# Moving block 0's query bound, the dense blocks' first transposes and the last block's start in a one-core transformer block

## The chip, the core and the metric

One core of a Trainium2 chip runs the kernel. Its engines have their own instruction streams, each executed in order, and wait for each other by semaphores: PE (TensorE, matrix products, with PEld as its weight loads), ACT (ScalarE), DVE (VectorE), POOL (GpSimd) and SP, which here issues most transfers. SBUF holds 128 partitions of data, and PSUM, in banks of 512 float32 per partition, takes what PE computes. The metric is the time of one execution on the device, in microseconds (us); the median of the runs is compared.

## What is computed

A transformer block on one sequence of 2048 tokens and 512 features, in float32: normalization, attention with 32 heads of 16 features that share one key and one value head, a residual, a second normalization and a gated feed-forward part (1792 inner features) with another residual.

```python
B, S, D, H, F = 1, 2048, 512, 32, 1792
q = (x @ wq).reshape(B, S, H, Dh).transpose(0, 2, 1, 3); k = x @ wk; v = x @ wv
p = softmax(einsum("bhqd,bkd->bhqk", q, k) * Dh ** -0.5)
o = einsum("bhqk,bkd->bhqd", p, v)          # heads side by side, then @ wo
h  = x + A(layernorm(x))                    # A: the lines above
h2 = h + (gelu(ln(h) @ w_gate) * (ln(h) @ w_up)) @ w_down
```

## The kernel before

**Precision.** Float32 operands are split into a rounded part and a rest (`split`, L106: the rounded copy, tile `...hi` or `...h`, then by a DVE subtraction the rest, `...lo` or `...l`), and a product is a sum of three PE products: high by high, high by low, low by high.

**Attention** runs over 4 blocks of 512 queries (b). In each, 8 groups (g) of 4 heads; in each group 16 chunks of 128 keys. For each key chunk there are two *scores*, numbered n in the program's order over everything (256 a block): a score is two PE matmuls into one of two PSUM tiles `s` (L329) and one exponential of 128x1024 on ACT, `p<-s` (L333). Two scores fill one tile p, which is numbered i = n // 2. `weigh` (L335) multiplies p with the values into the accumulator `acc` (eight PE instructions in the trace for each p), of which there is one: at the end of a group DVE copies it to `oT` (L350), and the next group's first `acc` waits for that copy. `oT` goes to DRAM, comes back transposed as `oc`, and is divided on DVE. Instead of a maximum, the softmax takes a bound: a row of the query operand holds m, computed from the norms of the queries and keys.

**Block 0** also computes the queries of all blocks (`project_q`, L170, a generator). Its loop (L800) goes over n; in every *cycle* of four scores it asks the generator for one step: `yield 3` is three products `pq`, and after a block's twelve such groups and their copies on DVE (`qh`, `ql`, `qs`) there is a sum of squares `pqn` (L218). Then DVE copies `qn` and takes its maximum `q2` (L223), in a later step POOL makes two factors `mm` (L227), and in another DVE makes the bound `m` and SP stores it (L245). These products share a single PSUM bank. While `work` is there (`given`, L809), the products of p with the values follow two at a time at the end of a cycle; without it, one by one (`finish(1)` at n % 4 == 2: the *plain* rhythm). The bound of the first heads of block 0 is made in the prologue (`urgent`). POOL meanwhile splits the dense weights and stores them to DRAM (`part_weights`).

**The dense part** of block b runs during the attention of block b + 1, as a generator too (`dense`, L517). The loop over chunks of 5 or 6 scores (L846) takes its steps by the table `kinds`: four "long" chunks for the output projection, one "gap", then the long ones of the feed-forward part. `start` (L570) makes the output projection `pp` for rows 0 and 1, then for rows 2 and 3 (a row is 128 tokens), with the transposes of row 0 in between. `residual` (L551) adds x to form `h`, takes the statistics (`st`, `mv`), POOL makes 1/sqrt (`rstd`, L120-121) and DVE the normalized `xn`; `x_transpose` (L562) transposes on PE into a bank `pxt`, from which `split` makes `x2h` and `x2l`. The first products of the feed-forward part, `pg` and `pu`, read all four rows of `x2h`. `duo` (L480) computes two products at once, each on half of the array's rows. Here three PSUM banks serve the products.

**The last block** has no attention to run beside: `start_tail` (L594) uses five further PSUM banks (`tail_bank`, L504) and full products (`solo`, L507). It interleaves its start with the last down products of block 2 (L899-909); the normalization takes a `shift` from POOL and runs on ACT (`on_act` in `layer_norm`, L113-131).

ACT, PE and POOL (L135) and, in the loops, SP and DVE keep the order in which the program writes their instructions.

Of the kernel before, what the change touches and what calls it, by code (L numbers as in the profile page):

```python
# [14 lines left out]
ALU = mybir.AluOpType  # L15
# [27 lines left out]
def kernel(  # L43
# [69 lines left out]
    def layer_norm(sb, xn, src, key, on_act=False):  # L113

        st = sb.tile([P, 6], F32, tag="st", bufs=4, name=f"st_{key}")
        mv = sb.tile([P, 2], F32, tag="mv", bufs=4, name=f"mv_{key}")
        nc.vector.bn_stats(st, src)
        nc.vector.bn_aggr(mv, st)  # L118
        rstd = sb.tile([P, 1], F32, tag="rstd", bufs=4, name=f"rstd_{key}")
        nc.gpsimd.tensor_scalar(rstd, mv[:, 1:2], EPS, None, op0=ALU.add)  # L120
        nc.gpsimd.tensor_tensor(rstd, rstd, power[:, 0:1], op=ALU.pow)
# [6 lines left out]
        nc.gpsimd.tensor_scalar(  # L128
            shift, mv[:, 0:1], rstd, -1.0, op0=ALU.mult, op1=ALU.mult
        )  # L130
        return partial(nc.scalar.activation, xn, src, AF.Identity, bias=shift, scale=rstd)
# [9 lines left out]
    def run(outer, first):  # L141
# [28 lines left out]
        def project_q(b, cs, eng, col):  # L170
# [46 lines left out]
            for i, c in enumerate(cs):  # L217
# [6 lines left out]
            yield 2  # L224

            mm = eb.tile([H, 3], F32, tag="mm", bufs=2, name=f"mm_{b}_{cs[0]}")
            nc.gpsimd.tensor_scalar(  # L227
                mm[:, 0:1], q2[:, col : col + 1], k2m, 1e-30, op0=ALU.mult, op1=ALU.add
            )
            nc.gpsimd.tensor_tensor(mm[:, 1:2], mm[:, 0:1], power[:H, 0:1], op=ALU.pow)  # L230
            nc.gpsimd.tensor_scalar(
                mm[:, 2:3], mm[:, 0:1], mm[:, 1:2], 0.5, op0=ALU.mult, op1=ALU.mult
            )
            nc.gpsimd.tensor_scalar(
                mm[:, 1:2], mm[:, 1:2], k2m, 0.5, op0=ALU.mult, op1=ALU.mult
            )
# [8 lines left out]
            nc.vector.tensor_scalar(m, qn, mm[:, 1:2], mm[:, 2:3], op0=ALU.mult, op1=ALU.add)  # L245
            hs = slice(cs[0] * HC, (cs[-1] + 1) * HC)
            nc.sync.dma_start(q_d[hs, 3 * DH, tsl].bitcast(F32), m[hs].bitcast(F32))
            yield 2

        ms = {}  # L250
# [3 lines left out]
        def later_q():  # L254
            second = project_q(1, range(DC), nc.vector, 1)
# [10 lines left out]
            check_bound(eb, k2m)  # L266
# [250 lines left out]
        def dense(b, tail=False):  # L517

            o_hi, o_lo = o_blk[b]
            eng = nc.scalar if tail else nc.vector  # L520
# [30 lines left out]
            def residual(t0):  # L551
# [7 lines left out]
                for scale in scaled:  # L559
                    scale()  # L560

            def x_transpose(t):  # L562
                bank = tail_bank if tail else psum1
                pt = bank(f"pxt_{b}_{t}").rearrange("p (c q) -> p c q", c=DC)
                for c in range(DC):
                    nc.tensor.transpose(pt[:, c, :], xns[t][:, c * P : (c + 1) * P], ident)  # L566
                sl = slice(t * P, (t + 1) * P)
                split(eng, xT_hi[:, :, sl], xT_lo[:, :, sl], pt)

            def start():  # L570
                yield from project(0)
                residual(0)
# [3 lines left out]
                second, turned = project(2), 0  # L576
                while True:
                    n = next(second, None)
                    if n is None:
                        break  # L580
                    if n == CUT:
                        yield EDGE
                        x_transpose(0)
                        turned = 1
                    yield n
                for t in range(turned, 2):
                    x_transpose(t)
                residual(2)
                yield GAP
                x_transpose(2)  # L590
                x_transpose(3)
                yield CUT

            def start_tail():  # L594
# [39 lines left out]
                for t in range(1, TB):  # L634
                    norm(t)
                for t in range(TB - 1):
                    scaled[t]()
                yield HOLD
                x_transpose(0)
                scaled[TB - 1]()  # L640
                x_transpose(1)
                yield 3
                x_transpose(2)
                x_transpose(3)
# [104 lines left out]
        gates = []  # L749
# [43 lines left out]
        with tc.manual_schedule(engines={mybir.EngineType.SP, mybir.EngineType.DVE}):  # L793
            parts = None
# [5 lines left out]
            while n < lead:  # L800
# [45 lines left out]
        for c in range(LEAD[0], (NB - 1) * NG * len(SIZES)):  # L846
# [18 lines left out]
            for j, share in enumerate(shares):  # L865
# [23 lines left out]
            finish(sum(e[5] < n - 1 for e in pend) if cg < len(SIZES) - 1 else len(pend))  # L889
            if outs:  # L890
# [337 lines left out]
```

## Time and profile before

| what | value |
|---|---|
| median of 3 runs | 1466.33 us (1466.04 to 1467.09) |
| profiled execution, its own time | 1464.85 us |
| its span, first to last instruction | 1462.9 us |
| DVE busy | 538.5 us (37%) |
| POOL busy | 222.2 us (15%) |
| PE in the chain that ended last | 76% of the span |
| ACT in that chain | 16% |

The profile is of one execution. A busy time is the time in which an engine had an instruction under way. A row of a timeline has start, duration, engine, line of the kernel, operation, tiles out<-in without their numbers, shape, count, and in brackets how long the engine had been idle and which instruction of which engine ended that. A window's row has its borders and length, then busy time and count for PE, PEld, DVE, ACT and POOL, and last the granted share of PE's clock, the share of the DMA engines in use and their GB/s. Where only some instructions are asked for, the engines without any are left out. The chain that ended last is followed back from the last instruction, at each step to what released it.

### The profile page before, as it was taken

To read this page: it belongs to the slowest core of one execution; us is meant where nothing else is said; L and a number is where in the kernel's file an instruction comes from. 1 tells how busy PE (TensorE), PEld (TensorE's weight loads), DVE (VectorE), ACT (ScalarE), POOL (GpSimd) and SP (SyncE) were. 2 spreads that over 40 slices of the span, in tenths; PEclk is the share of its full clock that TensorE was granted. 3 is DMA by queue.
4 is the path that set the end of the run, shared out by engine and by line. 5 is a ranking of instruction groups with operands and counts; after the bars stand their busy time and mean duration, and the time that the engine had idled before them with its cause. 6 is when DMAs were issued, how large, how long until landed. Compare 5 with 4: busy or idle time off the path is not lost.

```text
span 1462.9 us, 24764 instructions
## 1 busy us (share of the span) xinstructions
PE 1413.6 (97%) x10420; PEld 748.4 (51%) x10420; DVE 538.5 (37%) x925; ACT 1040.0 (71%) x1147; POOL 222.2 (15%) x305
## 2 busy tenths in 40 slices
PE   6999999999999999999999999999899999999998
PEld 5533333334555555554555555554455555556886
DVE  7412231313251424333251423423242332426665
ACT  6699999996777777776777777777677777772000
POOL 5477677611000000000000000000000000001000
PEclk9999999999999999999999999999999999999999
DMA  4465766641323332212332332203333232333552
GB/s 153 150 202 192 223 219 221 213 151 60 116 92 105 113 112 84 85 56 98 129 108 88 113 112 84 84 30 113 112 113 112 84 112 75 126 120 112 199 183 81
DMA packets 58863, 180.54 MB, mean 123 GB/s; under 512 B 8540, under 2 KB 8540, under 8 KB 51544
## 3 DMA queue, kind: packets, MB, share of 16 engines
q1 hardware_dynamic: 48912, 144.79, 29.1%
q0 software_dynamic: 9760, 34.08, 7.0%
q8 instruction: 84, 1.38, 0.4%
q14 instruction: 35, 0.29, 0.1%
q10 hardware_dynamic: 72, 0.00, 0.0%
HBM read 131.13 MB, written 47.71 MB: 122 GB/s over the span
## 4 chain that ended last, share of the span: by engine, by line
PE 76%; ACT 16%; DVE 3%; issue 3%; POOL 1%; DMA 0%; SPq 0%; ACTq 0%; POOLq 0%; DVEq 0%
PE acc L337 32%; PE s L329 17%; ACT p L333 16%; PE pd L490 5%; PE pu L490 5%; PE pg L490 4%; PE pq L180 3%; PE pg L512 3%; PE pd L512 3%; PE pu L512 3%; PE pp L490 1%; PE pxt L566 0%; PE pk L1015 0%; DVE x2h L110 0%; DVE x2l L111 0%
## 5 line engine op out<-in xcount | busy, mean ns | idle before, releaser
L333 ACT ACTIVATE p<-s 128x1024 f32<-128x1024 f32 x1024 | 969.2, 1042 | 274.4 <-PE s L329 273.9
L337 PE MATMUL acc<-p,v_sb 128*32 128x512 f32 x4096 | 492.8, 599 | 4.4 <-DVE oT L350 4.4
L329 PE MATMUL s<-qg,kaug 50*128 50x512 f32 x1984 | 394.9, 437 | 18.6 <-ACT p L333 15.1
L329 PEld LDWEIGHTS s<-qg,kaug 50*128 50x128 f32 x1984 | 170.9, 184 | 307.7 <-ACT p L333 192.0
L337 PEld LDWEIGHTS acc<-p,v_sb 128*32 128x32 f32 x4096 | 111.0, 109 | 247.1 <-issue 232.8
L490 PE MATMUL pg<-x2h,w 64*128 64x512 f32 x672 | 231.7, 391 | 3.0 <-DVE x2h L110 3.0
L490 PE MATMUL pu<-x2h,w 64*128 64x512 f32 x672 | 231.8, 391 | 0.0
L120 POOL TENSOR_SCALAR rstd<-mv 128x1 f32<-128x1 f32 x16 | 3.5, 218 | 1018.4 <-DVE mv L118 1018.2
L490 PEld LDWEIGHTS pg<-x2h,w 64*128 64x128 f32 x672 | 124.7, 186 | 15.2 <-DVE x2h L110 4.2
L490 PE MATMUL pg<-x2l,w 64*128 64x512 f32 x336 | 131.5, 391 | 0.7 <-DVE x2l L111 0.7
L490 PE MATMUL pu<-x2l,w 64*128 64x512 f32 x336 | 131.5, 391 | 0.0
L490 PEld LDWEIGHTS pu<-x2h,w 64*128 64x128 f32 x672 | 124.7, 186 | 11.1
L490 PE MATMUL pd<-w,gh 64*128 64x512 f32 x672 | 105.4, 391 | 0.0
L679 ACT ACTIVATE ga<-ga 128x512 f32<-128x512 f32 x56 | 36.2, 647 | 87.9 <-DVE ga L674 87.9
L671 DVE COPY g<-pg 128x512 f32<-128x512 f32 x56 | 38.5, 688 | 126.7 <-PE pg L490 121.1
L490 PEld LDWEIGHTS pd<-w,gh 64*128 64x128 f32 x672 | 63.3, 185 | 14.7 <-issue 0.7
L680 DVE SCALAR_TENSOR_TENSOR ga<-ga,g 128x512 f32<-128x512 f32 x56 | 38.8, 692 | 79.8 <-ACT ga L679 79.8
L490 PEld LDWEIGHTS pg<-x2l,w 64*128 64x128 f32 x336 | 62.3, 186 | 9.1 <-DVE x2l L111 1.6
L490 PE MATMUL pd<-w,gl 64*128 64x512 f32 x336 | 66.5, 392 | 0.0
L490 PEld LDWEIGHTS pu<-x2l,w 64*128 64x128 f32 x336 | 62.3, 186 | 7.3
L498 DVE COPY mark_pu<-pu 128x1 f32<-128x1 f32 x42 | 6.6, 158 | 159.3 <-PE pu L490 159.3
L707 DVE TENSOR_TENSOR h<-h,pd 128x512 f32<-128x512 f32 x48 | 30.8, 684 | 90.2 <-PE pd L490 90.2
(226 smaller groups left out, 1307.3 us busy)
## 6 DMA issues: line engine op xcount, KB each, us to landing
w<-w_d SPq DMA_DIRECT2D x84, 1024.0 KB
qg<-q_d SPq DMA_DIRECT2D x62, 200.0 KB
q_d<-qh SPq DMA_DIRECT2D x32, 256.0 KB
acc_d<-oT SPq DMA_DIRECT2D x32, 256.0 KB
oc<-acc_d SPq DMA_DIRECT2D x128, 64.0 KB
w_d<-w_0b POOLq DMA_DIRECT2D x14, 512.0 KB, 5.9
w_d<-w_1b POOLq DMA_DIRECT2D x14, 512.0 KB, 3.5
x<-in_A_x_dram SPq DMA_DIRECT2D x16, 256.0 KB
```

The lines of the kernel that those rows point to most:

```text
L120: nc.gpsimd.tensor_scalar(rstd, mv[:, 1:2], EPS, None, op0=ALU.add)
L180: nc.tensor.matmul(pq, wt[:, d, c * P : (c + 1) * P], xt[:, d, :], start=(n == 0), stop=(n == 3 * DC - 1),)
L329: nc.tensor.matmul(s[:, a, :], kaug[rows, kc * P : (kc + 1) * P], qg[rows, u, :], start=True, stop=True,)
L333: nc.scalar.activation(p[:, 2 * u : 2 * u + 2, :], s, AF.Exp, scale=SCALE)
L337: nc.tensor.matmul(acc[32 * j : 32 * j + 32, :], v_sb[:, kc, :], p[:, j, :], start=(kc == 0), stop=(kc == KC - 1), skip_group_check=True,)
L490: nc.tensor.matmul(banks[k], lhsT[rows], rhs[rows], start=(turn == 0 and i == 0), stop=(turn == 1 and i == n - 1), skip_group_check=True,)
L498: nc.vector.tensor_copy(mark, banks[1][:, :1])
L512: nc.tensor.matmul(bank, lhsT, rhs, start=(i == 0), stop=(i == len(ts) - 1))
L671: nc.vector.tensor_copy(g, pg)
L679: nc.scalar.activation(a, a, AF.Tanh, scale=GELU_A * GELU_C)
L680: nc.vector.scalar_tensor_tensor(a, a, 1.0, g, op0=ALU.add, op1=ALU.mult)
L707: nc.vector.tensor_tensor(hs[t], hs[t], pd, op=ALU.add)
```

## The change

Three things are moved; all products and exponentials stay.

- **Block 0.** `project_q` hands the factors and the bound of a later block to a list `after`, with the number of steps after which each is due (2 and 4, counted from the step of the sum of squares, which counts as the first), and goes on with the next products at once. `later_q` works the list off behind the products. `given` falls when the products have ended, not when the bound has.
- **Start of the dense part, blocks 0 to 2.** DVE's work on rows 2 and 3 (`residual(2)`) comes before the split of row 1, and the scaling to `xn` and that split wait in a list `behind` until the chunk's last weighing has been written (and with it, at a group's end, the copy to `oT`). The transposes of rows 2 and 3 stand behind the second score of the gap chunk instead of its end, and DVE makes both `x2h` before both `x2l`.
- **Start of the last block.** `shift` is a DVE instruction ahead of the scaling; row 2's transpose takes a bank of the other pool; `x2h` of rows 0 and 1 goes from ACT to DVE; the copies of `pp` into `h` come earlier on ACT, two of them between the scalings.

```diff
@@ layer_norm
-        nc.gpsimd.tensor_scalar(
-            shift, mv[:, 0:1], rstd, -1.0, op0=ALU.mult, op1=ALU.mult
-        )
-        return partial(nc.scalar.activation, xn, src, AF.Identity, bias=shift, scale=rstd)
+        def scale():
+            nc.vector.scalar_tensor_tensor(
+                shift, mv[:, 0:1], -1.0, rstd, op0=ALU.mult, op1=ALU.mult
+            )
+            nc.scalar.activation(xn, src, AF.Identity, bias=shift, scale=rstd)
+        return scale
@@ project_q
             nc.vector.tensor_reduce(q2[:, col : col + 1], qn, axis=AX.X, op=ALU.max)
-            yield 2
...
             if urgent:
+                yield 2
+                factors()
...
-            yield 0
-            nc.vector.tensor_scalar(m, qn, mm[:, 1:2], mm[:, 2:3], op0=ALU.mult, op1=ALU.add)
...
+            after.extend([[2, factors], [4, bound]])
             yield 2
@@ later_q
+            for said in later_products():
+                for entry in after:
+                    entry[0] -= 1
+                while after and after[0][0] <= 0:
+                    after.pop(0)[1]()
+                yield said
+            while after:
+                yield 0
+                after.pop(0)[1]()
+                yield 0
+            check_bound(eb, k2m)
@@ dense: residual, x_transpose
-                for scale in scaled:
-                    scale()
+                return scaled
...
-            def x_transpose(t):
-                bank = tail_bank if tail else psum1
+            def x_turn(t):
+                bank = tail_bank if tail and t != 2 else psum1
...
-                split(eng, xT_hi[:, :, sl], xT_lo[:, :, sl], pt)
+                if tail and t >= 2:
+                    first_part = partial(nc.scalar.activation, hi, pt, AF.Copy)
+                else:
+                    first_part = partial(nc.vector.tensor_copy, hi, pt)
+                return first_part, partial(
+                    nc.vector.tensor_tensor, lo, pt, hi.bitcast(F32), op=ALU.subtract
+                )
@@ dense: start
-                for t in range(turned, 2):
-                    x_transpose(t)
-                residual(2)
+                parts = x_turn(1)
+                behind.extend([*residual(2), *parts])
                 yield GAP
-                x_transpose(2)
-                x_transpose(3)
+                two = [x_turn(t) for t in (2, 3)]
+                for i in range(2):
+                    for parts in two:
+                        parts[i]()
                 yield CUT
@@ dense: start_tail
-                for t in range(1, TB):
-                    norm(t)
-                for t in range(TB - 1):
-                    scaled[t]()
+                scaled[0]()
+                out(0)
+                norm(1)
+                norm(2)
+                scaled[1]()
+                out(1)
+                norm(3)
+                scaled[2]()
                 yield HOLD
-                x_transpose(0)
-                scaled[TB - 1]()
-                x_transpose(1)
+                parts = x_turn(0)
+                parts[0]()
+                scaled[3]()
+                parts[1]()
+                for part in x_turn(1):
+                    part()
                 yield 3
...
-                for t in range(TB):
-                    nc.scalar.activation(hs[t], pps[t], AF.Copy)
+                out(2)
+                out(3)
@@ the loops
-                    given = work is not None
-                for _ in range(RAMP.get(n, n > 7 and n % 4 == 3) if given else 0):
-                    if next(work, None) is None:
-                        work = None
+                    given = work is not None and said > 0
+                for _ in range(RAMP.get(n, n > 7 and n % 4 == 3) if work is not None else 0):
+                    said = next(work, 0)
+                    if said == 0 and not after:
+                        drain()
...
+                if kind == "gap" and j == 1:
+                    said = next(work)
...
             finish(sum(e[5] < n - 1 for e in pend) if cg < len(SIZES) - 1 else len(pend))
+            while behind:
+                behind.pop(0)()
```

More of the change, by code (lines that the diff above doesn't have):

```diff
@@ L575, in start @@
                 yield CUT
[L576 to L580, printed above, removed]
+                second = project(2)
+                for n in second:
                     if n == CUT:
                         yield EDGE
-                        x_transpose(0)
-                        turned = 1
+                        for part in x_turn(0):
+                            part()
                     yield n
-                for t in range(turned, 2):
-                    x_transpose(t)
-                residual(2)
+                parts = x_turn(1)
+                behind.extend([*residual(2), *parts])
                 yield GAP
-                x_transpose(2)
-                x_transpose(3)
+                two = [x_turn(t) for t in (2, 3)]
+                for i in range(2):
+                    for parts in two:
+                        parts[i]()
                 yield CUT
@@ L747, in finish @@
                     evacuate(pb, pg, pacc)
-        gates = []
+        gates, behind = [], []
         def open_gates():
@@ L793, in run @@
         with tc.manual_schedule(engines={mybir.EngineType.SP, mybir.EngineType.DVE}):
-            parts = None
+            parts, said = None, 3
             if first:
```

48 lines of the change are left out of this document (30 added, 18 removed).

## The prediction

> **What bounds the kernel now.** I read the page first: its busy shares, then its costliest group.
>
> ```profile
> PE 1413.6 (97%) x10420; PEld 748.4 (51%) x10420; DVE 538.5 (37%) x925; ACT 1040.0 (71%) x1147; POOL 222.2 (15%) x305
> L333 ACT ACTIVATE p<-s 128x1024 f32<-128x1024 f32 x1024 | 969.2, 1042 | 274.4 <-PE s L329 273.9
> ```
>
> Through three quarters of the chain of waits PE is the last to finish. The exponentials (ACT) wait 273.9 us for scores, and one takes 1.04 us. The change adds no PE work and removes none, so only time in which PE waits, or runs at less than its rate, can be won. It lies in three places.
>
> First block 0, by the busy times of three windows: a stretch of loop cycles with a product, one without products in the rhythm that goes with them, one after the products.
>
> ```profile
> 205.96:271.11 65.15, 65.15 (x434) 24.98 (x433) 14.66 (x19) 60.35 (x65) 49.43 (x57) 1.00 0.67 220
> 275.27:287.17 11.90, 9.54 (x74) 3.10 (x74) 5.12 (x9) 11.31 (x13) 7.42 (x11) 1.00 0.52 183
> 291.47:320.38 28.91, 28.91 (x196) 8.45 (x192) 0.69 (x1) 28.91 (x33) 7.88 (x10) 1.00 0.33 111
> ```
>
> The windows run from the start of one exponential to the start of another, so the ACT counts hold one too many: 64, 12 and 32 exponentials. Four of them (one cycle) take 65.15/16 = 4.07 us with a product and PE busy throughout, 11.90/3 = 3.97 us in the empty cycles, where PE is busy 9.54 of 11.90 us, and 28.91/8 = 3.61 us in the plain rhythm, where ACT is always busy.
>
> Second, the first dense block's start in blocks 1 to 3. PE in block 2, in order of time (start, duration, idle before):
>
> ```profile
> 683.02 0.39 PE L490 MATMUL pp<-wo_hi,o_lo 64*128 64x512 f32 x2
> 683.34 0.65 PE L566 MATMUL pxt<-ident,xn 128*128 128x128 f32 x4
> 683.92 2.78 PE L337 MATMUL acc<-p,v_sb 128*32 128x512 f32 x24
> 686.63 0.73 PE L329 MATMUL s<-qg,kaug 50*128 50x512 f32 x4
> 690.65 1.41 PE L337 MATMUL acc<-p,v_sb 128*32 128x512 f32 x8 [1.82 <-DVE oT L350]
> 693.14 2.17 PE L337 MATMUL acc<-p,v_sb 128*32 128x512 f32 x8
> 695.67 1.09 PE L566 MATMUL pxt<-ident,xn 128*128 128x128 f32 x8
> 698.43 0.49 PE L490 MATMUL pg<-x2h,w 64*128 64x512 f32 x1 [1.00 <-DVE x2h L110]
> 699.50 0.39 PE L490 MATMUL pg<-x2h,w 64*128 64x512 f32 x1
> ```
>
> DVE beside it:
>
> ```profile
> 684.03 0.69 DVE L110 CAST x2h<-pxt 128x512 fp32r<-128x512 f32 x1 [6.47 <-PE pxt L566]
> 685.36 1.28 DVE L554 TENSOR_TENSOR h<-pp,xb 128x512 f32<-128x512 f32 x2
> 688.45 0.55 DVE L560 TENSOR_SCALAR xn<-h,mv,rstd 128x512 f32<-128x512 f32 x1 [0.20 <-POOL rstd L121]
> 689.45 0.55 DVE L560 TENSOR_SCALAR xn<-h,mv,rstd 128x512 f32<-128x512 f32 x1 [0.46 <-POOL rstd L121]
> 689.91 0.68 DVE L350 COPY oT<-acc 128x512 f32<-128x512 f32 x1
> ```
>
> PE waits three times: for the copy oT that stands last on DVE, then for the split of the late transposes (x2h), and in between it runs slowly, 2.17 us for the eight matmuls of acc.
>
> Third, the last block's start, where the third and fourth transposes wait for x2l (rows below).
>
> **Block 0.** The bound of the queries leaves the cycle of the products. Counted in the order of instructions, before has nine cycles without a product: two behind each of four sums of squares, and one more at the end, which all keep the rhythm of the products. After moves every later product up into these; one empty cycle is left, and the last eight, after the products, get the plain rhythm. The products themselves cost 4.07 us wherever they stand. So the gain is 9 x 3.97 - (3.97 + 8 x 3.61) = 2.9 us; the transition costs the same, wherever it comes: I take 2.8. Bounds: 3.2 (nine plain cycles), 2.0 (a third of it lost to a changed DVE order).
>
> What moves with it: on SP, each load of qg now follows one group of three stores of qh more or less than before. It is wanted seven cycles (7 x 4.07 = 28 us) after it is issued, so this is covered. On POOL the four instructions of the bound stand two to five weight parts earlier; they may hold the parts up, but POOL's 7.88 us in the third window above are the last of them, and their reader, the dense products, comes later. On DVE the bound itself now stands ahead of product copies, which is the slow rival below.
>
> **The start of the dense block.** Block 2 in the new order. DVE adds h first, when the products end (683.02 + 0.39 = 683.41): 683.45 in place of 685.36, 1.91 earlier. By the old distances (3.09 and 4.09 us from h to the two xn, POOL's part included) the xn could start at 686.54 and 687.54. But oT is now ahead of them and waits for acc, which ends at 683.92 + 2.78 = 686.70: oT 686.74 to 687.43, xn to 687.98 and 688.50. The transposes of both, which before followed five scores later, now stand in PE's order behind the second score, which ends at 686.63 + 0.73 = 687.36. So PE waits 0.7 us, works on them until 689.15 (0.65 us after the second xn), and the scores behind them are 0.8 us later than before. But now oT is done, and so are x2h and x2l: six DVE operations of 0.69 us from 688.5, by 692.7. Five more scores follow, at the pace of the exponentials, which I take as 1.06 us each with small waits (0.91 is the plain rhythm): 689.1 + 5.3 = 694.4 for the first gate product pg. Before, the third pair of products starts at 699.50; without the waits of the first two pairs, and 0.23 us for each pair, that is a start of 699.04. The gain is 4.6 us. Bounds: 5.4 at 0.91 us for a score, 2.9 at 1.4, the pace with a wait for acc at each score.
>
> Block 3 is the same stretch: from the scores to the third pair 12.91 us against block 2's 12.87, so 4.6 again.
>
> ```profile
> 1024.06 0.73 PE L329 MATMUL s<-qg,kaug 50*128 50x512 f32 x4
> 1036.97 0.39 PE L490 MATMUL pg<-x2h,w 64*128 64x512 f32 x1
> ```
>
> In block 1 the gap falls inside a group of heads, with no oT in it:
>
> ```profile
> 354.10 0.40 PE L490 MATMUL pp<-wo_hi,o_lo 64*128 64x512 f32 x2
> 358.93 0.75 PE L329 MATMUL s<-qg,kaug 50*128 50x512 f32 x4
> 367.96 0.39 PE L490 MATMUL pg<-x2h,w 64*128 64x512 f32 x1
> ...
> 357.09 1.28 DVE L554 TENSOR_TENSOR h<-pp,xb 128x512 f32<-128x512 f32 x2
> 361.18 0.55 DVE L560 TENSOR_SCALAR xn<-h,mv,rstd 128x512 f32<-128x512 f32 x1 [0.45 <-POOL rstd L121]
> ```
>
> h moves from 357.09 to 354.55, the second xn from 361.18 to 358.64, before the score at 358.93 is done (0.5 us): the transposes run from 359.45 to 360.5 (1.09), four scores follow, pg starts at 360.5 + 4 x 1.06 = 364.7 in place of 367.96 - 0.46 = 367.5. Gain 2.8; bounds 3.4 (0.91) and 1.4 (1.4).
>
> **The clock in the gap.** Windows of 3.41 us, a pair of each block; the third number from the end of a row is the granted clock:
>
> ```profile
> 687.84:691.25 3.41, 1.09 (x10) 0.34 (x10) 2.07 (x5) 2.28 (x3) 1.49 (x3) 1.00 0.00 0
> 691.25:694.67 3.42, 3.42 (x18) 0.87 (x12) 0.00 (x0) 1.85 (x2) 0.00 (x0) 0.50 0.34 119
> 1025.76:1029.17 3.41, 1.59 (x12) 0.44 (x12) 1.69 (x3) 1.79 (x2) 1.00 (x3) 1.00 0.08 32
> 1029.17:1032.58 3.41, 3.41 (x12) 0.72 (x12) 0.00 (x0) 1.94 (x2) 0.00 (x0) 0.50 0.31 107
> 363.57:366.98 3.41, 2.40 (x18) 1.24 (x14) 2.08 (x4) 1.73 (x3) 0.00 (x0) 1.00 0.00 0
> 366.98:370.39 3.41, 3.19 (x26) 2.47 (x28) 0.59 (x1) 1.75 (x3) 0.00 (x0) 1.00 0.02 5
> ...
> 363.57:366.98 3.41, 1.09 (x8) 0.85 (x8) 1.00 0.00 0
> ```
>
> After a window with PE busy 32% (block 2) or 47% (block 3) the clock is halved for the next one. In block 1, busy 70% (the last row counts its transposes alone, 1.09 us), it stays whole. My new gap holds idle PE of 0.7, 0.45 and 0.55 us in 7 us, over 65% busy in any 3.41 us, so I count it at the full clock.
>
> The Trainium skill speaks against that: "TensorE: Matmul & The Clock Gate", Part 4, says that a transpose does not count as PE work for the clock in the way other matmuls do; Part 1, that an idle window of about 3.4 us halves the clock. Block 1's row disagrees on the first: without transposes it is (2.40 - 1.09)/3.41 = 38% busy, less than block 3's 47%, and kept the clock. By that rule the new gap would be near 50% and might be halved again, and the sum 3.4 us less.
>
> **The last block's start.** PE, then ACT and DVE:
>
> ```profile
> 1335.85 1.46 PE L566 MATMUL pxt<-ident,xnp 128*128 128x128 f32 x8
> 1339.18 0.66 PE L566 MATMUL pxt<-ident,xnp 128*128 128x128 f32 x4 [0.98 <-DVE x2l L111]
> 1341.96 0.50 PE L512 MATMUL pg<-x2h,w 128*128 128x512 f32 x1
> ...
> 1337.13 0.78 ACT L637 ACTIVATE xnp<-pp,shift,rstd 128x512 f32<-128x512 f32 x1 [0.54 <-POOL shift L128]
> 1333.35 0.29 DVE L111 TENSOR_TENSOR o_lo<-oc,o_hi 128x128 fp32r<-128x128 f32 x1
> ```
>
> The third transpose waits for a bank that x2l frees; after gives it a bank of another pool, and it starts behind its xn (337.13 + 0.78, some 0.2 later by the shift on DVE: 1338.1) and the down products, at 1338.35. The fourth waits for its xn, whose shift now stands behind a DVE copy of x2h: xn 1338.25 to 1339.03, transpose to 1339.7, x2h on ACT to 1340.35, pg at 1340.5. The gain is 1.4 us. The first shift moves behind o_lo, 0.6 later (1333.64 plus a short operation), but its transpose starts only at 1335.85, behind down products, which hide it. Bounds: 2.0 and 0.
>
> **The sum.** 2.8 + 2.8 + 4.6 + 4.6 + 1.4 = 16.2 us. The profiled execution took 1464.85 us with a span of 1462.9, so the profile's own forecast is a span of 1446.7; its time lies 1.5 us below the median of the runs (1466.33), against which I set the forecast: 1450.1.
>
> **Rivals.** (a) The clock is halved again in blocks 2 and 3: half of 3.41 us each, 1453.5. For it the rows at 32% and 47%, against it block 1's.
> (b) The change does not shorten the gap as it says: the transposes hold up the scores as much as they advance the products, and each dense start gains only the 1.0 us wait before pg and, in blocks 2 and 3, the halved clock's 1.7. Then 2.8 + 1.4 + 1.0 + 2 x 2.7 = 10.6: 1455.7. For it PE's strict order; against it the DVE rows, by which both xn are ready 6 us before the old transposes.
> (c) Slower: in block 0 the bound waits on DVE for POOL, and product copies now stand behind it, with one PSUM bank for the products.
>
> ```profile
> 272.28 0.68 DVE L223 TENSOR_REDUCE q<-qn 32x1 f32<-32x512 f32 x1
> 282.85 0.88 DVE L245 TENSOR_SCALAR m<-qn,mm 32x512 fp32r<-32x512 f32 x1 [6.60 <-POOL mm L234]
> ```
>
> From the maximum (272.96) to the bound's start is 9.9 us here, POOL's factors being late. After leaves three cycles, 12.2 us, plus some 2 us until the bank is wanted. From a lag of 14 us each further us is lost; to be slower in all, it takes 16 + 3 us more, over three blocks 6.4 each, so a lag of 20 us, twice the measured one, and the time would be above 1469. Nothing shows that.
>
> **Chances.** The forecast 0.73, in its own range of 1447.5 to 1452.5; (a) 0.09; (b) 0.12; (c) 0.03; no net change, with (b) and half of (c) together, 0.03. A measurement of this kernel tells about 0.2%, 2.9 us, from no change. Faster by more is forecast, (a) and (b): 0.94; within it 0.03; slower 0.03. The range for 8 in 10 reaches from all upper bounds but a little (16.2 + 3.1, 1447.0) to the edge of (b): 1447 to 1456.
>
> **What would show it.** Right: exponentials four to 3.61 us from about 255 us on; in blocks 2 and 3 no acc waiting for oT, eight acc matmuls at 1.06 us, pg 7.8 us after the gap's first scores in place of 11.8 (698.43 - 686.63), and no window at 0.50 there; in the tail no transpose waiting for x2l, pg 1.4 us sooner. Wrong: PE waiting for xn by much more than 0.7 us, a clock of 0.50 behind the gap, or qh waiting for m in block 0.

## The result and the profile after

| what | before | after |
|---|---|---|
| median of 4 runs | 1466.18 us (1465.71 to 1467.09) | 1449.44 us (1449.19 to 1450.38) |
| ratio after / before, 95% | | 0.9886 [0.9869, 0.9903] |
| profiled execution, its own time | 1464.85 us | 1449.60 us |
| its span | 1462.9 us | 1447.8 us |

The time fell by 16.7 us by the medians and by 15.2 us by the two profiled executions, to 0.7 us below the forecast of 1450.1. First the page of the changed kernel: PE's row and its costliest group.

```profile
PE 1413.6 (98%) x10420; PEld 750.3 (52%) x10420; DVE 538.4 (37%) x931; ACT 1038.1 (72%) x1145; POOL 221.8 (15%) x301
L362 ACT ACTIVATE p<-s 128x1024 f32<-128x1024 f32 x1024 | 968.3, 1060 | 261.6 <-PE s L358 261.2
```

PE is as busy as before to 0.1 us, with as many instructions. By this sum only idle time of PE has gone; the exponentials wait 12.7 us less for scores.

Where the time went is seen best between the same exponentials of both kernels, since there are 1024 of them in the same order. The table has the time from the start of one to the start of another, by their numbers n (counted from 0), from the traces; "last part" runs to the span's end. The two right columns belong to two experiments below.

| stretch (exponentials) | before | after | won | forecast | e2_dense | e7_weigh_later |
|---|---|---|---|---|---|---|
| block 0 (1 to 272) | 272.87 | 269.82 | 3.05 | 2.8 | 272.40 | 269.83 |
| block 1's gap (288 to 304) | 22.73 | 20.20 | 2.53 | 2.8 | 20.20 | 19.57 |
| block 2's gap (544 to 555) | 18.58 | 14.55 | 4.03 | 4.6 | 14.54 | 13.35 |
| block 3's gap (800 to 811) | 18.64 | 14.54 | 4.10 | 4.6 | 14.54 | 13.36 |
| last part (from 1023) | 146.35 | 144.58 | 1.77 | 1.4 | 147.02 | 144.39 |
| the four stretches between | 929.54 | 929.59 | 0.0 | 0 | 929.52 | 929.39 |

All that was won was won in the five places of the forecast: 15.5 us, of which the span keeps 15.1, since exponential 1 starts 0.3 us later than in the profile of before. Two further profiles of before (e10 and e11 below) show how far one kernel's stretches differ between executions: block 0 took 272.30 and 272.86 us there, the last part 146.69 and 147.20. So the 3.05 and 1.77 are good to some 0.6 and 0.9 us.

**Block 0.** The same three kinds of windows as shown of before: cycles with a product, the one empty cycle, the plain rhythm (16 cycles, 1, 8):

```profile
186.46:251.74 65.28, 64.70 (x432) 24.54 (x430) 20.23 (x24) 60.36 (x66) 47.61 (x54) 1.00 0.68 220
251.74:255.70 3.96, 3.66 (x30) 1.06 (x30) 0.69 (x1) 3.77 (x5) 1.57 (x3) 1.00 0.98 345
259.39:288.30 28.91, 28.91 (x196) 8.47 (x192) 6.97 (x11) 28.91 (x34) 24.78 (x32) 1.00 0.65 197
```

A cycle takes 65.28/16 = 4.08 us with a product, 3.96 empty, and 28.91/8 = 3.61 plain. The plain rhythm begins with a cycle at 255.70, and costs the same with three times the weight parts on POOL (24.78 us busy instead of 7.88).

**The start of the dense block.** PE in block 2, then DVE beside it:

```profile
681.38 0.73 PE L358 MATMUL s<-qg,kaug 50*128 50x512 f32 x4
682.72 1.11 PE L594 MATMUL pxt<-ident,xn 128*128 128x128 f32 x8 [0.61 <-DVE xn L942]
683.77 0.50 PE L358 MATMUL s<-qg,kaug 50*128 50x512 f32 x2
684.19 1.06 PE L366 MATMUL acc<-p,v_sb 128*32 128x512 f32 x8
685.19 0.76 PE L358 MATMUL s<-qg,kaug 50*128 50x512 f32 x4
685.87 1.98 PE L366 MATMUL acc<-p,v_sb 128*32 128x512 f32 x8
687.78 0.73 PE L358 MATMUL s<-qg,kaug 50*128 50x512 f32 x4
689.40 0.50 PE L358 MATMUL s<-qg,kaug 50*128 50x512 f32 x2 [0.89 <-ACT p L362]
689.74 0.40 PE L519 MATMUL pg<-x2h,w 64*128 64x512 f32 x1
...
681.52 0.69 DVE L379 COPY oT<-acc 128x512 f32<-128x512 f32 x1 [0.42 <-PE acc L366]
682.13 0.99 DVE L942 TENSOR_SCALAR xn<-h,mv,rstd 128x512 f32<-128x512 f32 x2
685.56 1.28 DVE L626 TENSOR_TENSOR x2l<-pxt,x2h 128x512 fp32r<-128x512 f32 x2
```

The wait of acc for oT and that of pg for x2h are gone, PE waits 0.61 us for xn, and x2l is done at 686.84, three microseconds before pg reads it. From the gap's first scores to pg it is 689.74 - 681.38 = 8.36 us (before 11.80, forecast 7.8). The clock stays whole through the gap; three windows side by side, of the same length as before:

```profile
679.60:683.01 3.41, 2.80 (x27) 0.93 (x20) 2.92 (x7) 0.99 (x2) 1.53 (x4) 1.00 0.00 0
683.01:686.42 3.41, 3.41 (x26) 1.41 (x24) 3.38 (x7) 2.67 (x4) 0.00 (x0) 1.00 0.37 127
686.42:689.83 3.41, 2.52 (x16) 0.83 (x14) 0.42 (x1) 2.75 (x4) 0.00 (x0) 1.00 0.46 147
```

**The last block's start.** Its last transposes on PE, the first pg, and the scalings of rows 2 and 3 on ACT:

```profile
1324.82 1.09 PE L594 MATMUL pxt<-ident,xnp 128*128 128x128 f32 x8
1326.73 1.64 PE L541 MATMUL pg<-x2h,w 128*128 128x512 f32 x6
...
1323.65 1.51 ACT L133 ACTIVATE xnp<-pp,shift,rstd 128x512 f32<-128x512 f32 x2
```

Both transposes run in one piece without a wait, and pg follows 1326.73 - 1303.22 = 23.51 us after the start of exponential 1023 (before 1341.96 - 1316.60 = 25.36): 1.85 us sooner.

### The profile page after: what moved, and what is told of

It reads as the page before. It is cut to its first block, busy times and chain, and to the rows that moved or that the text cites. A ratio compares the mean times of both kernels' runs of the same rounds, so it can differ in the third digit from the quotient of the medians.

```text
span 1447.8 us, 24764 instructions
## 1 busy us (share of the span) xinstructions
PE 1413.6 (98%) x10420; PEld 750.3 (52%) x10420; DVE 538.4 (37%) x931; ACT 1038.1 (72%) x1145; POOL 221.8 (15%) x301
## 4 chain that ended last, share of the span: by engine, by line
PE 76%; ACT 18%; issue 3%; DVE 1%; DMA 0%; POOL 0%; SPq 0%; ACTq 0%; DVEq 0%
PE acc L366 31%; ACT p L362 18%; PE s L358 17%; PE pd L519 5%; PE pu L519 5%; PE pg L519 4%; PE pq L184 4%; PE pg L541 3%; PE pd L541 3%; PE pu L541 3%; PE pp L519 1%; PE pk L1068 1%; PE pxt L594 1%; PE pt L1058 0%; PE pqn L222 0%
## 5 line engine op out<-in xcount | busy, mean ns | idle before, releaser
L395 DVE RECIPROCAL oc<-oc 128x128 f32<-128x128 f32 x64 | 56.0, 919 | 24.6 <-DMA oc<-acc_d 20.7
```

The lines of the kernel that those rows point to most:

```text
L395: nc.vector.reciprocal(oc[:, 1, sl], oc[:, 1, sl])
```

## The experiments

Beside the first four the kernel before had a median of 1466.67 us (25 runs), beside the next four 1466.96 (9 runs), beside e9 to e11 1465.72 (10 runs). Ratios are to the kernel before.

**One part of the change at a time.** e1 has block 0's part alone, e2 the dense start, e3 the last block's start. The excerpts, here and for e4 and e5 against the kernel before, show the lines that tell the parts apart.

```diff
# e1_block0
+            after.extend([[2, factors], [4, bound]])
...
+                    given = work is not None and said > 0
# e2_dense
+                behind.extend([*residual(2), *parts])
...
+                if kind == "gap" and j == 1:
+                    said = next(work)
# e3_tail
+            nc.vector.scalar_tensor_tensor(
+                shift, mv[:, 0:1], -1.0, rstd, op0=ALU.mult, op1=ALU.mult
+            )
...
+                bank = tail_bank if tail and t != 2 else psum1
```

> The kernel before with the change of block 0 alone. Theory (the parts act apart, and block 0 wins nine cycles' worth of rhythm): 2.8 us off before, about 1463.4; block 1's first score some 3 us earlier, everything behind it as before, the two windows at half clock still there. Rival (the time won in block 0 is waited for later, because the weights that POOL splits are not ready): within 0.5 us of before.

> The kernel before with the change of the dense blocks' start alone. Theory: 2.5 us in block 1, 4.1 in blocks 2 and 3, so 10.7 off before, about 1455.5, and no window at half clock. Rival (part of this came from block 0's earlier end): less than 9 us off.

> The kernel before with the change of the last block's start alone. Theory: the third transpose no longer waits for x2l, 1.4 to 1.9 us off before, about 1464.5. Rival (the last block is bound further on, by the gates on DVE and ACT): within 0.5 us of before.

| kernel | median, us | ratio, 95% |
|---|---|---|
| e1_block0 | 1464.17 (1461.98 to 1465.64, 10 runs) | 0.9983 [0.9973, 0.9993] |
| e2_dense | 1454.34 (1453.75 to 1458.11, 4 runs) | 0.9922 [0.9896, 0.9948] |
| e3_tail | 1464.62 (1461.62 to 1467.70, 10 runs) | 0.9980 [0.9967, 0.9994] |

By the medians the parts win 2.5, 12.3 and 2.1 us, together 16.9, the whole change 16.7: they add, and none hides another. e2's 12.3 are 1.6 more than the 10.7 that its expectation took from one pair of profiles. In each trace the stretches that the edit leaves alone lie where the three profiles of before have them (block 0 at 272.30 to 272.88 us, the last part at 146.35 to 147.20), to 0.1 us, with one exception. In e1 and e3, whose code for block 1's gap is that of before, this gap took 24.28 and 24.29 us instead of 22.73. The clock was at half there, after a window that in before had left it whole. In e1:

```profile
362.13:365.54 3.41, 2.18 (x16) 1.23 (x16) 2.42 (x4) 1.94 (x2) 0.00 (x0) 1.00 0.02 5
365.54:368.95 3.41, 3.41 (x20) 2.70 (x18) 0.00 (x0) 1.29 (x2) 0.00 (x0) 0.50 0.00 0
```

So a profile's clock in this gap is one outcome of several, which e10 and e11 take up.

**The two halves of the dense start.** e4 only moves the transposes on PE (the order on DVE is that of before), e5 only reorders DVE.

```diff
# e4_pe_place
+                if kind == "gap" and j == 1:
+                    said = next(work)
# e5_dve_order
+                behind.extend([*residual(2), *parts])
```

> The kernel before with nothing changed but PE's place for the transposes of rows 2 and 3: behind the gap's second score, while DVE keeps the order of before (split of row 1, then h, then xn, then oT). Theory (DVE's order carries the gain, the place on PE alone makes PE wait for xn): PE waits about 1.7 us for the first xn and again for the second, pg 2.4 us sooner in blocks 2 and 3 and 0.6 in block 1, 5.4 us off, 1460.8, if the clock stays whole; with a clock halved behind the wait in blocks 2 and 3, 2 us off, 1464.2. Rival (the place on PE is the whole gain): 1455.5.

> The kernel before, with the dense start's new order on DVE alone (residual of rows 2 and 3 ahead of row 1's split, xn and the split behind the copy oT); the transposes of rows 2 and 3 stay at the end of the gap chunk, block 0 and the last block are as before. Theory (both halves of the dense start are needed: DVE's order removes the wait for oT and with it the half clock, PE's place removes the wait for x2h before pg): in blocks 2 and 3 the 1.8 us for oT and the 1.5 to 1.7 us of half clock go, the 1.0 us before pg stays; some 3.3 us each, almost nothing in block 1, where no oT stands in the gap: 6.6 off, about 1459.9 beside 1466.5. Rival 1 (DVE's order is the whole gain of the dense start): 1454.3, what the two halves together measured. Rival 2 (it is the place on PE that carries it, the order adds nothing by itself): 1466, no change.

e4: 1462.96 us (1459.72 to 1469.23, 10 runs), ratio 0.9975 [0.9958, 0.9992]. e5: 1460.60 us (1459.08 to 1464.10, 6 runs), ratio 0.9958 [0.9945, 0.9971]. They win 3.7 and 6.4 us, both together 12.3 (e2): 2.2 us come only with both. PE in block 2's gap, first of e4:

```profile
688.32 0.63 PE L565 MATMUL pxt<-ident,xn 128*128 128x128 f32 x4 [1.78 <-DVE xn L593]
689.23 1.12 PE L565 MATMUL pxt<-ident,xn 128*128 128x128 f32 x4 [0.28 <-DVE xn L593]
```

then of e5:

```profile
692.64 1.09 PE L565 MATMUL pxt<-ident,xn 128*128 128x128 f32 x8
694.68 0.50 PE L490 MATMUL pg<-x2h,w 64*128 64x512 f32 x1 [0.28 <-DVE x2h L597]
695.37 0.47 PE L490 MATMUL pu<-x2h,w 64*128 64x512 f32 x1 [0.19 <-DVE x2l L597]
```

In e4 the transposes come early and wait for xn as long (1.78 us) as acc had waited for oT; in its profile the clock is halved from 688.90 on for 6.8 us, and block 2's gap is 18.55 us, as before (block 3's is 17.71 with 3.4 us at half clock, block 1's 22.18 at the whole clock). In e5 the waits for oT are gone and block 2's and 3's gaps are 15.94 and 15.95, with the clock whole. What is left to after's 14.55 is pg, which still follows right behind late transposes. So behind DVE's new order the place on PE is worth 1.4 us more (2.3 in block 1).

That doesn't make the place on PE worthless by itself. e4's ten runs fall apart by their mean granted clock: four took 1459.7 to 1460.8 us at 0.999, the clock of the changed kernel's runs, and six took 1462.2 to 1469.2 at 0.993 to 0.998. Its expectation had put 1460.8 for a whole clock and 1464.2 for a halved one, and both came. So the place alone wins some 6 to 7 us where the clock stays whole, about as much as the order alone. What the order brings to it is that the wait goes, and with it the halved clock. Only one of the ten, of the six, has a profile, so it is not shown that half clock in the gaps is all that separates the two groups. Rival (b), that the new place holds the scores up as much as it helps, fell with e2 and the table above: it left the three dense starts 1.0 + 2 x 2.7 = 6.4 us, and they won 10.7 in the profile and 12.3 by e2's medians.

**The clock is a matter of phase.** The kernel before, unchanged, was profiled twice more.

> The kernel before, unchanged, profiled a second time. Theory (the window in which PE's work is counted for its clock runs freely, so the same idle stretches fall into it differently at each execution): the gaps of blocks 2 and 3 are halved in clock again, and block 1's may be too; if it is, its gap takes 24.3 in place of 22.7 us. All other segments within 0.2 us of the first profile's, the last part of the kernel within 1 us. Rival: the outcome is a property of the program and the clock record repeats: halved at the two places of the first profile alone.

> The same as the run above, a third profile of the kernel before. Theory: among the three profiles the places with half clock differ, and with them the gaps (22.7 or 24.3 us in block 1, and in blocks 2 and 3 up to 3.4 us of half clock each), while the segments between stay equal to 0.2 us. Rival: all three have the same two places.

Windows of e10 (blocks 2 and 3), then of e11 (block 1); the third number from the end is the granted clock:

```profile
686.00:689.41 3.41, 1.33 (x10) 0.48 (x6) 2.69 (x8) 2.68 (x3) 1.71 (x4) 1.00 0.00 0
689.41:696.23 6.82, 6.11 (x22) 1.37 (x22) 0.66 (x2) 2.12 (x3) 0.00 (x0) 0.50 0.37 109
1023.91:1027.33 3.42, 2.04 (x18) 0.48 (x6) 2.91 (x7) 1.97 (x3) 1.52 (x4) 1.00 0.00 0
1027.33:1034.15 6.82, 5.41 (x20) 1.08 (x20) 1.15 (x2) 2.83 (x3) 0.18 (x1) 0.50 0.27 90
```

```profile
364.54:367.95 3.41, 2.18 (x15) 1.22 (x15) 2.67 (x4) 1.94 (x2) 0.00 (x0) 1.00 0.02 5
367.95:371.36 3.41, 3.41 (x18) 2.67 (x18) 0.00 (x0) 1.02 (x1) 0.00 (x0) 0.50 0.00 0
```

| profile of before | block 1's gap | block 2's | block 3's | span |
|---|---|---|---|---|
| first | 22.73, whole clock | 18.58, 3.4 us at half | 18.64, 3.4 us at half | 1462.94 |
| e10 | 22.70, whole clock | 19.84, 6.8 us at half | 19.54, 6.8 us at half | 1464.84 |
| e11 | 24.27, 3.4 us at half | 18.59, 3.4 us at half | 18.59, 3.4 us at half | 1465.16 |

One program, three outcomes: the theory held for the gaps, the rival fell. Block 0 of e10, 0.6 us shorter than in the first profile, missed the 0.2 expected of the other stretches. A hit costs 1.5 us in block 1, and a second window in a row 0.9 to 1.3. The first profile, on which the forecast stood, was the luckiest of the three. The changed kernel was at the whole clock in all three gaps in its profile, as were e2, e6, e7, e8 and e9. The mean granted clock was 0.999 or 1.0 in each of the 16 runs of after, e6, e7 and e8, and at most 0.996 in the 25 runs of before beside the first four. One of e2's four runs, 1458.11 us, had 0.996; it wasn't profiled, and where its clock was halved is open. It need not be a gap: in e5's profile the clock was at half for 3.4 us from 1335.61 on, in the last block's start of before, which e2 has too, behind a window with PE busy 1.78 of 3.41 us, and the last part took 148.47 us.

**Rival (c), brought about.** e9 is the changed kernel with POOL's factors made late: two steps further back, behind 8 us more of weight parts, and with the power computed 13 times.

```diff
-            after.extend([[2, factors], [4, bound]])
+            after.extend([[4, factors], [4, bound]])
...
+                for _ in range(1 if urgent else 13):
                     nc.gpsimd.tensor_tensor(
                         mm[:, 1:2], mm[:, 0:1], power[:H, 0:1], op=ALU.pow
                     )
```

> The changed kernel with rival (c) brought about: in block 0 the bound's factors are put behind the fourth step instead of the second (8 us more of weight parts ahead of them on POOL), and POOL makes the power of each factor 13 times over, same result (12 x 0.67 = 8.0 us more). Theory: DVE's bound then waits for POOL with copies of products behind it, and loses from the moment the single PSUM bank is wanted again. Block 1's bound: factors done about 129.3 us, bound to 130.2, qh and ql to 131.6, while the next products want the bank at 128.7: 2.9 us lost. Block 2's: factors 201.2, ql to 203.5, bank wanted at 198.0: 5.5 lost. Block 3's has no copies behind it and costs nothing. Together 8.4: 1457.9 beside 1449.4. Rival: the copies may be late without cost, because products come only every fourth score: 1449.5; or POOL's 24 us hold the weight parts up past the first dense block: more than 1460, with block 1's segments longer.

1469.97 us (1466.89 to 1472.35, 7 runs), ratio 1.0024 [1.0009, 1.0038]: it loses 20.5 us to the changed kernel and is slower than before by a little. The bounds on DVE, then PE where it waits, then two windows:

```profile
128.69 0.89 DVE L249 TENSOR_SCALAR m<-qn,mm 32x512 fp32r<-32x512 f32 x1 [18.48 <-POOL mm L242]
210.39 0.79 DVE L249 TENSOR_SCALAR m<-qn,mm 32x512 fp32r<-32x512 f32 x1 [12.15 <-POOL mm L242]
288.54 0.88 DVE L249 TENSOR_SCALAR m<-qn,mm 32x512 fp32r<-32x512 f32 x1 [16.51 <-POOL mm L242]
...
130.22 3.64 PE L367 MATMUL acc<-p,v_sb 128*32 128x512 f32 x16 [4.72 <-DVE oT L380]
212.56 0.80 PE L184 MATMUL pq<-xT_hi,wq_hi 128*128 128x512 f32 x1 [6.02 <-DVE ql L111]
...
125.70:129.12 3.42, 0.00 (x0) 0.00 (x0) 0.43 (x1) 1.89 (x3) 2.99 (x7) 1.00 0.00 0
129.12:139.32 10.20, 9.10 (x35) 2.93 (x39) 3.27 (x5) 3.88 (x4) 9.23 (x12) 0.50 0.78 235
```

The wait was expected at 2.9 and 5.5 us and measured at 4.72 and 6.02. In block 1 it was not the bank that came first but oT, which also stands behind the bound on DVE. Its profiled execution is the shortest of the seven, and 17.5 us longer than that of after from exponential 1 to 256 (272.27 against 254.76). The two waits are 10.7 of it; the other 6.8 fits the half clock after each, 10.2 and 6.8 us long, whose most is half of 17.0. That price was in no expectation. The third bound waits just as long and costs nothing, since no product copies stand behind it.

**The pace of the scores.** After the transposes, the scores took 689.74 - 683.77 = 5.97 us up to pg, where the forecast had 5.3. The rows of PE above have 2 + 4 + 4 + 2 matmuls s there, two for each score, so these are six scores (exponentials 546 to 551) at 1.00 us each. The forecast and the expectation of e7 count five, and e7's therefore has 1.19 us for each; the sum of 5.97 stays the same. Between the scores stand the products acc. In after the second of them starts at 685.87, when exponential 547, which it reads, has just begun (685.72); half of its matmuls start only at 686.80, behind that exponential's end, and the scores behind them in PE's order come so late that exponential 549 waits 0.66 us for its own. ACT, by its exponentials 547 and 548, then 549 to 551:

```profile
685.72 1.94 ACT L362 ACTIVATE p<-s 128x1024 f32<-128x1024 f32 x2 [0.34 <-PE s L358]
688.32 2.86 ACT L362 ACTIVATE p<-s 128x1024 f32<-128x1024 f32 x3 [0.66 <-PE s L358]
```

Against the changed kernel, e6 puts xn ahead of oT; e7 writes the products of p with the values one score later in the gap; e8 does both.

```diff
# e6_xn_first
-                behind.extend([*residual(2), *parts])
+                for step in residual(2):
+                    step()
+                behind.extend(parts)
# e7_weigh_later
-                    finish(sum(e[5] < n - 1 for e in pend))
+                    finish(sum(e[5] < n - 1 - (kind == "gap") for e in pend))
```

> The changed kernel, with one thing turned: the two scalings to xn of rows 2 and 3 stand on DVE ahead of the copy oT, and only row 1's split stays behind it. Theory (the wait of PE for xn in the gap, 0.6 us in blocks 2 and 3, is the price of putting xn behind oT, and oT is not wanted for a while): the wait goes, some 0.5 us each in blocks 2 and 3, nothing in block 1; 1.0 us off the changed kernel's 1449.4, 1448.4, within what runs can tell, but the profile's two gaps go from 14.55 to about 14.05. Rival: oT then comes later by the wait for the two rstd of POOL, the first acc of the next group waits for it as it did before the change, and the gaps are 14.5 or longer; a halved clock there would make it 1.5 more each.

> The changed kernel, with the products of p with the values written one score later within the gap chunk. Theory (the five scores between the transposes and pg come at 1.19 us each in place of the forecast 1.06 because acc, in PE's order between them, waits for the exponential just begun): the scores then come at the pace of the exponentials, 0.92 to 1.06, so 0.6 to 1.3 us less in each of the three gaps (14.55 to about 13.5 in blocks 2 and 3, 20.2 to 19.4 in block 1): 1446.5 beside 1449.4. Rival: acc only moves to behind the gap and what it saves there is paid in the next chunk; the sum of the segments around the gap is unchanged, 1449.4.

> The changed kernel with both: the two xn ahead of oT, and the weighing one score later within the gap chunk. Theory: both gains add, about 1445.5 to 1446, and the gaps of blocks 2 and 3 are near 13.0. Rival: with oT later, the first acc of the new group waits whatever its place, and this is no faster than the one of the two that gains, or than the changed kernel (1449.4).

| kernel | median, us (4 runs each) | ratio, 95% | gaps of blocks 1, 2, 3 |
|---|---|---|---|
| after | 1449.44 (1449.19 to 1450.38) | 0.9886 [0.9869, 0.9903] | 20.20, 14.55, 14.54 |
| e6_xn_first | 1449.10 (1449.01 to 1449.76) | 0.9880 [0.9864, 0.9897] | 20.20, 14.35, 14.37 |
| e7_weigh_later | 1446.25 (1445.65 to 1447.14) | 0.9862 [0.9845, 0.9878] | 19.57, 13.35, 13.36 |
| e8_both | 1446.69 (1445.75 to 1447.89) | 0.9863 [0.9846, 0.9879] | 19.56, 13.17, 13.18 |

PE in e7, from behind the transposes in block 2:

```profile
682.54 0.74 PE L358 MATMUL s<-qg,kaug 50*128 50x512 f32 x4
683.21 1.06 PE L366 MATMUL acc<-p,v_sb 128*32 128x512 f32 x8
684.22 0.50 PE L358 MATMUL s<-qg,kaug 50*128 50x512 f32 x2
685.13 0.50 PE L358 MATMUL s<-qg,kaug 50*128 50x512 f32 x2 [0.41 <-ACT p L362]
685.56 1.06 PE L366 MATMUL acc<-p,v_sb 128*32 128x512 f32 x8
686.56 0.91 PE L358 MATMUL s<-qg,kaug 50*128 50x512 f32 x4
687.31 0.39 PE L519 MATMUL pg<-x2h,w 64*128 64x512 f32 x1
```

The six scores now take 687.31 - 682.54 = 4.77 us, 0.80 each, and both acc go through in 1.06 us; in after the second took 1.98. The gaps of blocks 2 and 3 and the median came as e7's theory had them (about 13.5 and 1446.5), and its reason, acc waiting in PE's order, does not hang on the count. The next stretches are no longer for it (the table above), so the time isn't paid back: e7 gains 3.2 us more by the medians, and its slowest run is 2.0 us below the fastest of after. It beats both kernels. e6 fell short: 0.2 us in each gap for 0.5 expected, since the second xn then waits for POOL's second rstd and the transposes wait for it again:

```profile
682.36 0.66 PE L594 MATMUL pxt<-ident,xn 128*128 128x128 f32 x4 [0.19 <-DVE xn L622]
```

In e8 the two add in the gaps, but its last part is 145.79 us to e7's 144.39 (144.4 to 145.0 in the other profiles with the new last block). There pg waits 1.2 us for weights; after, e6 and e7 have no such wait, e2 has one of 0.4 us, and one profile doesn't tell whether it is the edit's doing:

```profile
1335.14 2.08 PE L541 MATMUL pg<-x2h,w 128*128 128x512 f32 x8 [1.20 <-DMA w<-w_d]
```

## Why the prediction was right, step by step

- **What bounds the kernel.** Right: PE's busy time didn't move, and what was won was won in the places named.
- **Block 0, 2.8 us: 3.05 in the profile, 2.5 by e1's medians.** Right, and by its steps: one empty cycle is left, and the plain ones take 3.61. That POOL's parts, SP's loads and the copies don't mind the new order held too: PE's waits from 60 to 290 us come to 0.7 us (7.3 before), and the stretches behind are unchanged.
- **The dense start, 2.8 + 4.6 + 4.6 = 12.0: measured 2.5 + 4.0 + 4.1 = 10.7.** The mechanism was right, up to the transposes to a tenth: they were forecast to start 4.65 us after the products' end (688.06 - 683.41) and did so after 4.56 (682.72 - 678.16). The step behind them was wrong: "Five more scores follow". Six do in blocks 2 and 3, as shown above, and in block 1 five (exponentials 296 to 300), where the forecast had four. The new place is the second score of a gap chunk of six scores (five in block 1), and pg comes behind the second score of the next chunk. Six and five scores at the forecast's 1.06 us would have been 6.4 and 5.3 us, and by the forecast's own sum a gain of about 3.5 + 3.5 + 1.7, or 8.8. What made up for most of that is the other half of the term: the scores came faster than 1.06, at 5.97/6 = 1.00 in blocks 2 and 3, and at (362.24 - 357.65)/5 = 0.92 in block 1. Left are the 0.6 that blocks 2 and 3 miss, and the 0.3 of block 1. Two errors of opposite sign thus stand in this term, and that it came out only 1.3 us too high is in part luck. e7 tells what sets the pace: acc, in PE's order between the scores, waits for an exponential just begun, and the scores behind acc wait with it; with acc one score later each gap gets 0.6 to 1.2 us shorter.
- **The clock.** That the new gap keeps the whole clock was right; rival (a) fell in six profiles with this gap (after, e2, e6 to e9). The reason was half right. That block 1's gap, busy 70%, keeps the whole clock held for that phase of the windows alone: with the window 1 us further on, the same code is 64% busy and was followed by half (2.18 of 3.41 us, e11). Against the rule of the Trainium skill that was weighed there ("TensorE: Matmul & The Clock Gate", Part 4, transposes not counted as other matmuls are) speaks a window of before's last part, all of PE first, then its transposes alone:

```profile
1336.37:1339.78 3.41, 2.29 (x16) 1.32 (x14) 0.74 (x2) 2.75 (x5) 1.67 (x5) 1.00 0.00 0
...
1336.37:1339.78 3.41, 1.40 (x10) 0.84 (x8) 0.74 (x2) 1.18 (x2) 1.00 0.00 0
```

  It is 2.29/3.41 = 67% busy and, without transposes, (2.29 - 1.40)/3.41 = 26%; the clock stayed whole behind it. The window of e1 shown above is 2.18/3.41 = 64% busy, 59% without its 0.15 us of transposes, and was followed by half. With transposes counted the two stand in the right order, without them in the wrong one. Another pair stands the other way: e11's window, 49% busy without its 0.50 us of transposes, was followed by half, and e10's in the same gap (365.14 to 368.55), 2.17/3.41 = 64% busy with no transposes in it, was not. So how far transposes count stays open; that they count for nothing does not fit a window that kept the clock at 26%.
- **The last block, 1.4 us: 1.85 to the first pg.** The mechanism was right, and the term mis-sized is the fourth transpose: it was to wait for its xn, at 1339.03 - 1316.60 = 22.43 us after exponential 1023. The xn of rows 2 and 3 were done in one piece at 1323.65 + 1.51 = 1325.16, which is 21.94 after it, and the transpose ran through. e3 has 2.1 by the medians.
- **Rival (c).** The mechanism is real (e9). Its price was put as three blocks at a lag of 20 us each; it is two blocks at 18.5 and 21.9 (from the maximum's end to the bound), plus a half clock. The changed kernel stays clear of it: its longest lag is that of block 3, where no product copies are behind:

```profile
248.74 0.68 DVE L227 TENSOR_REDUCE q<-qn 32x1 f32<-32x512 f32 x1
264.12 0.53 DVE L248 TENSOR_SCALAR m<-qn,mm 32x512 fp32r<-32x512 f32 x1 [9.11 <-POOL mm L241]
```

- **The sum.** 16.2 forecast, 15.1 by the spans, 16.7 by the medians. The forecast missed 1.1 us of the profile: the dense starts came 1.3 short, the other two places 0.6 over, and exponential 1 started 0.3 us later. By the medians it was saved by what it didn't know: the other two profiles of before have more windows at half clock than the one that it started from (two more in e10, one in e11, with spans 1.9 and 2.2 us longer, 0.9 of e11's in the last part), and the changed kernel has none in its gaps. The agreement to 0.7 us is thus in part luck.

Not settled: some runs of before went to 1472 us, further than the hits of e10 and e11 reach. The three slowest beside the first four experiments (1469.44, 1471.03 and 1472.14 us) have a mean granted clock of 0.995, no lower than most of the others, so half clock doesn't explain them; none of them was profiled.

## What to carry to other kernels

A consumer's place in one engine's order and its producers' order on another engine belong together: look for both before counting a gain. By the medians they won 3.7 and 6.4 us alone and 12.3 together, and the place alone left a wait whose price changed from execution to execution (1459.7 to 1469.2 us). Count the work between two events from the program's order, and check the count in the trace's rows: one score too few was 1.06 us in each gap. Between two scores of a pipeline that waits on ACT, put only work whose inputs are older than the last exponential; one score more of distance was worth 3.2 us here. Where a profile shows a halved clock after a half-idle stretch, profile the same kernel again before pricing it: what one execution kept, the next may lose, and the gain of closing the stretch is a mean over phases.

## What the runs showed of the hardware that was not expected

- The clock's changes lie on a fixed grid: in e1 it was halved at 365.54, 689.81 and 1027.73 us, 324.27 = 95 x 3.413 and 337.92 = 99 x 3.413 us apart. By the Trainium skill ("TensorE: Matmul & The Clock Gate", Part 1) the window is 3413 ns and runs freely; the traces agree, since the place of this grid against the program differs between executions (half clock from 691.25 us on in the first profile of before, from 692.22 in e11, in the same gap).
- A window need not be idle to halve the clock. The clock went from whole to half behind windows of 0, 39, 60 and 64% busy in the rows above, and behind none of 67% or more in these profiles. There is no clean bound by busy share: e10's block 1 kept the clock behind 64%, and e4 had a window at 58% that cost nothing. Nor did one busy window always bring the clock back: in e10 a second window at half followed one that was 2.70 of 3.41 us busy, and in e9 a third followed one busy throughout.

```profile
357.80:361.21 3.41, 1.98 (x14) 0.67 (x14) 2.69 (x7) 2.05 (x2) 2.00 (x5) 1.00 0.04 14
361.21:364.62 3.41, 3.13 (x21) 1.28 (x22) 2.86 (x5) 1.53 (x2) 0.38 (x1) 1.00 0.00 0
```
